# A fused attention and feed-forward layer: gate/up phases alternated with attention phases, segment by segment

## The chip, the core and the metric

The kernel runs on one core of a Trainium2 chip. A core has a tensor engine (PE, matrix products; its weight loads are listed as PEld), a vector engine (DVE), a scalar engine with lookup tables for functions such as exp (ACT), a general engine (POOL) and a queue engine (SP) that mainly issues transfers. Each engine works through its own instructions in order and waits on semaphores for the others. Matrix products land in PSUM, a small accumulator memory; everything else is in SBUF or in DRAM. The metric is the device time of one execution in microseconds. The profile names the clock that was granted to PE; it can be halved.

## The reference

The input is a sequence of 2048 rows of width 448. It is normalised, goes through a segmented attention with a recurrent memory (16 heads of width 28, 4 segments of 512 rows), and through a gated feed-forward block of inner width 1792; the two results are multiplied and added to the input.

```python
x = A_x
xn = _layernorm(x, axis=-1)
s = _A_ref(xn, A_wq, A_wk, A_wv, A_wo, A_beta)
g = _silu(_B_ref(xn, B_w_gate, B_w_up, B_w_down))
return x + s * g
```

Within `_A_ref`, for each segment (phi(t) is t + 1 for positive t, else exp(t)):

```python
p = _softmax(logits, axis=-1)
a_dot = jnp.einsum('bhqk,bhkd->bhqd', p, vs)
pq = phi(qs)
num = jnp.einsum('bhld,bhde->bhle', pq, M)
den = jnp.einsum('bhld,bhd->bhl', pq, z)[..., None] + 1e-06
a_mem = num / den
o = g * a_mem + (1.0 - g) * a_dot
outs.append(o)
pk = phi(ks)
M = M + jnp.einsum('bhld,bhle->bhde', pk, vs)
z = z + jnp.einsum('bhld->bhd', pk)
```

`logits` are the scaled products of queries and keys of the same segment with a causal mask, and `_B_ref` is `_gelu(x @ w_gate) * (x @ w_up) @ w_down`.

## The kernel before

Everything runs on tiles of 128 rows; a segment is four such blocks (`NB`), the 16 heads are four groups (`G`) of four heads padded to 32 columns, the inner width is 14 chunks (`NFC`).

The program is written as a sequence of tile operations, and a scheduler sets the order of the instructions on each engine. It may move work ahead of work that stands earlier in the code. Tiles come from pools with a fixed number of buffers; a new tile of a name waits until the oldest buffer of that name is free. PSUM has three pools of two buffers each: `ps_s` (two banks a tile: scores, or the gate and up products), `ps_pv` (P times V sums, or down sums) and `ps_m` (everything else, tiles named `m`).

The program has two halves. The first, lines 316 to 341, does the attention of all four segments:

- `layer_norm(s)`, line 127: statistics on DVE, the power -1/2 on POOL (L137), transposes on PE (L144).
- `project(s)`, line 172: queries and keys of each group (L182), values (L198), keys by row (L206), and the phi functions through ACT's exp (L189, L209).
- `scores` and `pv`, lines 239 and 261: for each group three steps over the key blocks. PE computes scores (L248), ACT the exp (L252), POOL the causal mask (L255), PE the product with the values (L266). The product of one step is issued after the scores of the next (`pend`).
- `evac`, line 274: DVE copies the sum out of PSUM (L276) and SP writes the row sums to DRAM (`den`).
- `memory_read(s, g)`, line 280: the read of the memory for a group (L282).
- `normalise(s)`, line 284: the row sums come back (`dc`), DVE forms the reciprocals (L292, L295), they go to DRAM (`rdr`) and come back broadcast over 128 partitions (`rb`, L302, one transfer of 256 KB for each group and side). POOL then multiplies and adds (L309 for segment 0; L312, L313, L314 for the others) and leaves the result in `oT`. A segment after the first has two sides, the softmax and the memory.
- `update(s)`, line 217: the memory gains the segment's keys and values.

The second half, the loop that starts at L350, is the feed-forward of all segments and the end: for each segment 14 pairs of gate and up products (L358), gelu on ACT (L361), the product on DVE (L362) into `hT`; then for each block the down products (L367), the wo products of the attention (L371), silu on ACT (L374), a product on DVE (L375), the sum with the input on POOL (L376), and one transfer out per segment. Between the halves stand a barrier and the reuse of the first half's SBUF. `oT` and `xnT` hold all four segments.

A guard, lines 148 to 168, computes from the weights whether the scores can overflow an exp without a maximum; if they could, a general path (not run with these inputs) computes the result.

## Time and profile before

| what | us |
|---|---|
| median of three runs | 378.45 |
| lowest and highest run | 376.80, 379.18 |
| the profiled execution | 377.6 |
| its span in the profile | 375.8 |
| mean granted clock of PE | 0.869 of full |

The profile covers one execution. Its span runs from the first to the last recorded activity; the execution's own time is 1.8 us longer. In a row of a timeline the first two numbers are start and duration in us, then come engine, line, operation, output and input tiles with sizes, and the number of instructions that were merged; in square brackets stands how long the engine was idle before and what ended it. Neighbouring matmuls overlap, so a matmul's cost in a dense stretch is the distance from start to start. In a row of the costliest groups the two numbers after the first bar are the group's busy time in us and the mean of one in ns. In a row of windows the columns are the window and its length, then for each engine the busy time and the number of instructions, then PE's granted clock, the share of the transfer engines that was busy and GB/s.

### The profile page before, as it was taken

The page shows a single profiled execution, that of the slowest core. Times are in us where ns is not written, and L with a number is a line of the kernel's source. Part 1 is how long each engine was busy: PE and PEld are TensorE (multiplying, and loading weights), DVE is VectorE, ACT ScalarE, POOL GpSimd, SP SyncE. Part 2 cuts the span into 40 slices and gives each one's busy share as a digit, 9 for nine tenths or more (in the row PEclk, how much of TensorE's full clock was granted, in tenths as well). Part 3 has the DMA queues.
Part 4 walks back from the last instruction along what each step waited for, and adds up shares of the span by engine and source line. Part 5 has one row for each costly group of instructions (what it writes and reads, how often), then busy time and mean ns, then how long its engine had stood idle before and what let it go on. Part 6 is the DMA issues. An engine that isn't in the chain of part 4 may idle for free. (4 is left out here: it accounts for less than half of the span.)

```text
span 375.8 us, 4396 instructions
## 1 busy us (share of the span) xinstructions
PE 308.9 (82%) x1619; PEld 128.8 (34%) x1620; DVE 159.6 (42%) x297; ACT 146.4 (39%) x203; POOL 142.0 (38%) x207
## 2 busy tenths in 40 slices
PE   0356999995998924898346999999999999999992
PEld 0122343331423402223212244454445444544450
DVE  6827976872537703248221134312341234123420
ACT  1000589663456632437333723413333333333330
POOL 9800456337333187624579405661003100310021
PEclk9999999995559965559855589999999999999998
DMA  8991010011000122000220012613000300010001
GB/s 210 253 314 54 2 50 4 5 57 63 5 3 4 48 102 88 5 1 13 92 101 37 7 37 101 161 35 98 2 0 2 98 1 2 0 50 2 0 0 57
DMA packets 16964, 20.30 MB, mean 54 GB/s; under 512 B 2616, under 2 KB 12344, under 8 KB 16936
## 3 DMA queue, kind: packets, MB, share of 16 engines
q1 hardware_dynamic: 15472, 18.75, 16.2%
q10 hardware_dynamic: 1432, 1.20, 1.5%
q8 instruction: 14, 0.23, 0.3%
q14 instruction: 14, 0.11, 0.1%
q0 software_dynamic: 32, 0.00, 0.0%
HBM read 17.66 MB, written 2.29 MB: 53 GB/s over the span
## 5 line engine op out<-in xcount | busy, mean ns | idle before, releaser
L252 ACT ACTIVATE pt<-s 128x1024 bf16<-128x1024 f32 (+1 forms) x96 | 81.8, 881 | 93.4 <-PE s L248 66.7
L255 POOL TENSOR_SCALAR_AFFINE_SELECT pt<-pt 128x256 bf16<-128x256 bf16 x128 | 52.9, 432 | 64.2 <-ACT pt L252 63.4
L362 DVE TENSOR_TENSOR hT<-gl,s 128x512 bf16<-128x512 bf16 x56 | 38.2, 687 | 63.5 <-ACT gl L361 63.5
L358 PE MATMUL s<-xnT,wg_sb 112*128 112x512 bf16 x224 | 58.8, 386 | 0.1
L358 PE MATMUL s<-xnT,wu_sb 112*128 112x512 bf16 x224 | 58.4, 384 | 0.0
L361 ACT ACTIVATE gl<-s 128x512 bf16<-128x512 f32 x56 | 33.1, 597 | 63.5 <-PE s L358 63.5
L376 POOL TENSOR_TENSOR o_out<-sl,x_sb 128x448 bf16<-128x448 f32 x16 | 16.5, 1034 | 105.1 <-DVE sl L375 102.7
L266 PE MATMUL pv<-pt,vaug 128*32 128x128 bf16 (+3 forms) x256 | 37.7, 378 | 21.6 <-POOL pt L255 21.1
L248 PE MATMUL s<-qT,kT 32*128 32x128 bf16 (+3 forms) x256 | 43.0, 361 | 7.2 <-POOL mbd L234 5.0
L367 PE MATMUL pv<-wd_sb,hT 128*128 128x448 bf16 x224 | 44.3, 352 | 0.0
L358 PEld LDWEIGHTS <-wg_sb 112*128 112x128 bf16 x224 | 22.2, 99 | 27.3 <-issue 2.1
L358 PEld LDWEIGHTS <-wu_sb 112*128 112x128 bf16 x224 | 22.1, 99 | 27.1 <-issue 1.3
L367 PEld LDWEIGHTS <-hT 128*128 128x128 bf16 x224 | 21.9, 98 | 20.7
L182 PE MATMUL m<-xnT,wq_pad 112*128 112x512 bf16 x64 | 22.3, 468 | 6.9 <-DVE qT L186 5.5
L266 PEld LDWEIGHTS <-vaug 128*32 128x32 bf16 x256 | 11.2, 97 | 49.0 <-issue 47.0
L375 DVE TENSOR_TENSOR sl<-sl,m 128x448 f32<-128x448 f32 x16 | 9.9, 621 | 37.5 <-PE m L371 18.8
L312 POOL TENSOR_TENSOR oU<-oU,rb 128x512 f32<-128x512 f32 x12 | 15.2, 1266 | 20.9 <-DVE hT L362 12.4
L276 DVE COPY oU<-m 128x512 f32<-128x512 f32 x12 | 8.2, 690 | 33.7 <-PE m L282 14.9
L182 PE MATMUL m<-xnT,wk_pad 112*128 112x512 bf16 x64 | 22.0, 454 | 0.2 <-ACT phq_e L189 0.2
L248 PEld LDWEIGHTS <-kT 32*128 32x128 bf16 x256 | 10.7, 95 | 31.8 <-issue 29.2
L276 DVE COPY oU<-pv 128x512 f32<-128x512 f32 x16 | 11.0, 689 | 22.3 <-PE pv L266 20.8
L374 ACT ACTIVATE sl<-pv 128x448 f32<-128x448 f32 x16 | 8.7, 544 | 26.8 <-PE pv L367 26.8
(72 smaller groups left out, 291.3 us busy)
## 6 DMA issues: line engine op xcount, KB each, us to landing
rb<-rdr SPq DMA_DIRECT2D x28, 256.0 KB
x_sb<-in_A_x_dram SPq DMA_DIRECT2D x8, 448.0 KB
out_dram<-o_out SPq DMA_DIRECT2D x4, 448.0 KB
wg_sb<-in_B_w_gate_dram SPq DMA_DIRECT2D x1, 1568.0 KB
wu_sb<-in_B_w_up_dram SPq DMA_DIRECT2D x1, 1568.0 KB
wd_sb<-in_B_w_down_dram SPq DMA_DIRECT2D x1, 1568.0 KB
den<-oU SPq DMA_DIRECT2D x28, 8.0 KB
wq_raw<-in_A_wq_dram ACTq DMA_DIRECT2D x1, 392.0 KB
```

Source lines behind the costliest of these rows:

```text
L182: nc.tensor.matmul(out=pr[:], lhsT=wpad[nm][:, c, g * HG:(g + 1) * HG, :].rearrange("p h d -> p (h d)"), rhs=xnT[:, c, s, :], start=(c == ...
L248: nc.tensor.matmul(out=sp[:, j, c0:c0 + n], lhsT=kT[s][r, g, kb * P:(kb + 1) * P], rhs=qT[s][r, g, kb * P:L], start=True, stop=True)
L252: nc.scalar.activation(out=pt[:, :, 0:w], in_=sp[:, :, 0:w], func=ACT.Exp, scale=scale)
L255: nc.gpsimd.affine_select(out=v, in_=v, pattern=[[0, 2], [1, P]], compare_op=ALU.is_ge, fill=0.0, base=0, channel_multiplier=-1)
L266: nc.tensor.matmul(out=acc[i * HP:(i + 1) * HP, kb * P:L], lhsT=va[:, kb, g * HG + i, :], rhs=pts[i // 2][:, i % 2, c0:c0 + n], start=(kb ...
L276: nc.vector.tensor_copy(out=t[:], in_=ps[:])
L312: nc.gpsimd.tensor_tensor(out=o_a[:], in0=o_a[:], in1=rb[0][:], op=ALU.mult)
L358: nc.tensor.matmul(out=gu[:, i, :], lhsT=w_sb[:, c, fc * P:(fc + 1) * P], rhs=xnT[:, c, s, :], start=(c == 0), stop=(c == NDC - 1))
L361: nc.scalar.activation(out=gl[:], in_=gu[:, 0, :], func=ACT.Gelu_apprx_tanh)
L362: nc.vector.tensor_tensor(out=hT[:, fc, :], in0=gl[:], in1=gu[:, 1, :], op=ALU.mult)
L367: nc.tensor.matmul(out=d_ps[:, 0:D], lhsT=hT[:, fc, b * P:(b + 1) * P], rhs=wd_sb[:, fc, :], start=(fc == 0), stop=(fc == NFC - 1))
L376: nc.gpsimd.tensor_tensor(out=o_out[:, b, :], in0=sl[:], in1=xr[:, b, :], op=ALU.add)
```

## The change

The code is reordered so that the feed-forward of a segment runs between and beside the attention phases. The new main loop, in full:

```diff
+        layer_norm(0)
+        for _, f in project_units(0):
+            f()
+        oki = guard()
+        flip("exp")
+        for s in range(NSEG):
+            if s + 1 < NSEG:
+                if s > 0:
+                    load_x(s + 1)
+                layer_norm(s + 1)
+            if s < NSEG - 1:
+                gate_up(s)
+                flip("gelu")
+            if s == 2:
+                ok = nc.values_load(oki[0:1, 0:1], min_val=0, max_val=1)
+            pre = [(0.22, lambda g=g: memory_read(s, g)) for g in range(G)] if s > 0 else []
+            lists = []
+            if s < NSEG - 1:
+                lists.append(down_units(s))
+                lists.append(project_units(s + 1))
+            if s > 0:
+                lists.append(finish_units(s - 1))
+            if s < NSEG - 1:
+                pre.append((0.9, lambda: update(s)))
+            attention(s, pre + merge(*lists))
+            flip("exp")
+            normalise(s)
+        gate_up(NSEG - 1)
+        dn, fi = down_units(NSEG - 1), finish_units(NSEG - 1)
+        for b in range(NB):
+            for _, f in dn[3 * b:3 * b + 3] + fi[b:b + 1]:
+                f()
```

So segments 0, 1 and 2 have a gate/up phase, then an attention phase with fill; segment 3 has its attention directly after that of segment 2, and its gate/up behind it. `merge` interleaves the lists of units by their shares of the total; `attention` puts units between the steps:

```diff
+                    for pr in range(2):
+                        pts.append(scores(s, g, bk, pr))
+                        if pr == 0 and pend is not None:
+                            pend()
+                        n += 1
+                        while fill and done < tot * n / (6 * G):
+                            c, f = fill.pop(0)
+                            f()
+                            done += c
```

The units are the projections of the next segment (one unit for each L182, L198 and L206 group of before), the down products in pieces of five matmuls, and the end of the segment before (`finish_units`: wo products, product with the gate, sum with the input, and now one transfer in and one out per block). A down accumulator takes a `ps_m` tile in segments 0 to 2, and a `ps_pv` tile in segment 3. Silu is replaced by tanh, with the factor one half moved into `igate`:

```diff
-        nc.vector.tensor_scalar(out=igate[:], in0=igate[:], scalar1=1.0, scalar2=None, op0=ALU.add)
+        nc.vector.tensor_scalar(out=igate[:], in0=igate[:], scalar1=1.0, scalar2=2.0,
+                                op0=ALU.add, op1=ALU.mult)
...
-                sl = work.tile([P, D], F32, name="sl")
-                nc.scalar.activation(out=sl[:], in_=d_ps[:, 0:D], func=ACT.Silu)
-                nc.vector.tensor_tensor(out=sl[:], in0=sl[:], in1=a_ps[:, 0:D], op=ALU.mult)
-                nc.gpsimd.tensor_tensor(out=o_out[:, b, :], in0=sl[:], in1=xr[:, b, :], op=ALU.add)
...
+                    th = work.tile([P, D], F32, name="th")
+                    nc.scalar.activation(out=th[:], in_=d_ps[:, 0:D], func=ACT.Tanh, scale=0.5)
+                    t = blk.tile([P, D], F32, name="sg")
+                    nc.vector.scalar_tensor_tensor(out=t[:], in0=th[:], scalar=1.0,
+                                                   in1=d_ps[:, 0:D], op0=ALU.add, op1=ALU.mult)
```

ACT's functions are kept in phases: every exp of an attention phase is ordered behind the gelus before it and ahead of those after it.

```diff
+        def act(kind, **kw):
+            ins = nc.scalar.activation(**kw)
+            ins = getattr(ins, "ins", ins)
+            for p_ in prev["gelu" if kind == "exp" else "exp"]:
+                tc.add_manual_dep(ins, p_, ORDER, reason="one table at a time")
+            phase[kind].append(ins.name)
```

At the start, w_up goes to ACT's queue and w_gate stands directly ahead of the second segment's input on SP's; the guard moves behind the projections of segment 0; several memsets move from DVE to POOL and cover only the padding. `xnT`, `oT` and `hT` hold one or two segments instead of four, `oup` has 4 buffers instead of 5 for each side, and `pkb` one instead of two. The barrier between the halves is gone.

How this moves the instructions is shown at three places, before first and then now.

DVE at the start. BN_STATS on `x_sb` are the statistics of a segment's blocks, L140 and L193 the normalising, L145 and L198 the copies of the transposes, L186 and L217 those of the projections. Before:

```order
L140 TENSOR_SCALAR xn<-x_sb,mv,rstd 128x448
L168 TENSOR_REDUCE oki<-okh 1x1
L140 TENSOR_SCALAR xn<-x_sb,mv,rstd 128x448
L145 COPY xnT<-m 112x4x128 x2
L132 BN_STATS st<-x_sb 128x6 x2
L133 BN_AGGR mv<-st 128x2
L186 CAST qT<-m 128x512
```

Now (the fifth BN_STATS on DVE, the first of segment 1, is the second row):

```order
L193 TENSOR_SCALAR xn<-x_sb,mv,rstd 128x448 x2
L185 BN_STATS st<-x_sb 128x6
L198 COPY xnT<-m 112x4x128
L193 TENSOR_SCALAR xn<-x_sb,mv,rstd 128x448
L198 COPY xnT<-m 112x4x128
L193 TENSOR_SCALAR xn<-x_sb,mv,rstd 128x448
L198 COPY xnT<-m 112x4x128
L186 BN_AGGR mv<-st 128x2
```

The statistics of segment 1 stood behind the transposes of segment 0 and ahead of its projections; now the first of them stands ahead of the copies of the transposes.

POOL at the change from segment 1 to segment 2. The normalise operations of segment 1 are L312 to L314 before, L352 to L354 now; AFFINE_SELECT is the causal mask of segment 2. Before:

```order
L314 TENSOR_TENSOR oT<-oU_1011,oU_991 128x512
L312 TENSOR_TENSOR oU_1277<-oU_1277,rb_1310 128x512
L255 AFFINE_SELECT pt<-pt 128x2x128
L313 TENSOR_TENSOR oU_1058<-oU_1058,rb_1312 128x512
L255 AFFINE_SELECT pt<-pt 128x2x128
L314 TENSOR_TENSOR oT<-oU_1277,oU_1058 128x512
L255 AFFINE_SELECT pt<-pt 128x2x128 x24
```

Now:

```order
L354 TENSOR_TENSOR oT<-oU_1689,oU_1299 128x512
L352 TENSOR_TENSOR oU_1810<-oU_1810,rb_1844 128x512
L353 TENSOR_TENSOR oU_1304<-oU_1304,rb_1846 128x512
L354 TENSOR_TENSOR oT<-oU_1810,oU_1304 128x512
L295 AFFINE_SELECT pt<-pt 128x2x128 x2
L275 TENSOR_TENSOR macc<-macc,rb_2136 128x512
L276 CAST mbd<-macc 128x512
L295 AFFINE_SELECT pt<-pt 128x2x128 x4
```

The masks stood between the normalise operations; now all twelve normalise operations of segment 1 stand ahead of the first mask of segment 2.

PE at the wo products of segment 2 (L371 before, L398 now; the rows LDWEIGHTS are the weight loads, and `oT` is what normalise leaves). Before, where the first wo products of the program stand:

```order
L358 LDWEIGHTS wu_sb
L358 MATMUL s<-xnT,wu_sb 128x512
L371 LDWEIGHTS oT
L371 MATMUL m<-wo_sb,oT 128x448
L371 LDWEIGHTS oT
L371 MATMUL m<-wo_sb,oT 128x448
```

Now, in the attention of segment 3:

```order
L398 LDWEIGHTS oT
L398 MATMUL m<-wo_sb,oT 128x448
L305 LDWEIGHTS vaug_151
L305 MATMUL pv<-pt,vaug_151 32x256
L305 LDWEIGHTS vaug_151
L305 MATMUL pv<-pt,vaug_151 32x256
L288 LDWEIGHTS kT
L288 MATMUL s<-qT,kT 128x256
L398 LDWEIGHTS oT
L398 MATMUL m<-wo_sb,oT 128x448
```

The wo products stood in the feed-forward half, among gate and up products; those of segment 2 now stand among the last scores and P times V products of segment 3.

More of the change, by code (lines that the diff above doesn't have):

```diff
@@ L208, in project @@
[L208 to L215 removed]
+                    u.append((0.75, lambda b=b: ktok(b)))
@@ L363, in fast_path @@
-            o_out = op_.tile([P, NB, D], out.dtype, name="o_out")
-            for b in range(NB):
-                d_ps = ps_pv.tile([P, L], F32, name="pv")
-                for fc in range(NFC):
-                    nc.tensor.matmul(out=d_ps[:, 0:D], lhsT=hT[:, fc, b * P:(b + 1) * P],
-                                     rhs=wd_sb[:, fc, :], start=(fc == 0), stop=(fc == NFC - 1))
+                act("gelu", out=gl[:], in_=gu[:, 0, :], func=ACT.Gelu_apprx_tanh)
+                nc.vector.tensor_tensor(out=hT[s][:, fc, :], in0=gl[:], in1=gu[:, 1, :], op=ALU.mult)
```

402 lines of the change are left out of this document (218 added, 184 removed).

## The prediction

> **What bounds the kernel now.** I read the page first: the busy shares, the forty slices and the chain that ended last.
>
> ```profile
> span 375.8 us, 4396 instructions
> PE 308.9 (82%) x1619; PEld 128.8 (34%) x1620; DVE 159.6 (42%) x297; ACT 146.4 (39%) x203; POOL 142.0 (38%) x207
> PE   0356999995998924898346999999999999999992
> PEclk9999999995559965559855589999999999999998
> GB/s 210 253 314 54 2 50 4 5 57 63 5 3 4 48 102 88 5 1 13 92 101 37 7 37 101 161 35 98 2 0 2 98 1 2 0 50 2 0 0 57
> PE s L358 26%; PE pv L367 11%; PE m L371 3%; POOL o_out L376 1%; DVE sl L375 0%; PE pv L266 0%; POOLq L729 0%; DVEq L375 0%
> ```
>
> There are two halves. From about 215 us the tensor engine (PE) is full and at full clock: the feed-forward stage, priced by the chain. Before that, attention and projections leave PE with gaps and a halved clock.
>
> ```profile
> 221.65 20.72 PE s L358 x96
> 242.38 5.30 PE pv L367 x28
> 254.11 0.76 PE m L371 x4
> ```
>
> A gate/up matmul costs 20.72/96 = 0.216 us, a down matmul 5.30/28 = 0.189, four wo matmuls 0.76. A segment's gate/up is 112 x 0.216 = 24.2 us, its down 56 x 0.189 = 10.6, its wo 3.0. None of this gets cheaper.
>
> The stages of the first half, by windows (us; busy time of PE, PEld, DVE, ACT, POOL; granted clock):
>
> ```profile
> 47.00:75.00 28.00, 26.64 (x188) 10.60 (x186) 20.26 (x43) 22.54 (x30) 14.78 (x34) 1.00 0.08 20
> 100.00:110.00 10.00, 10.00 (x50) 2.40 (x51) 2.79 (x7) 6.14 (x8) 3.32 (x8) 0.50 0.00 1
> 175.00:200.00 25.00, 12.62 (x82) 4.75 (x84) 8.74 (x14) 9.45 (x12) 16.80 (x20) 0.70 0.23 86
> ```
>
> With projections to fill it PE is dense (first row); with only attention left (175 to 200) it is half idle. What holds it then is POOL, seen in the PE timeline:
>
> ```profile
> 35.64 0.39 PE L248 MATMUL s<-qT,kT 32*128 32x512 bf16 x1
> 37.25 1.04 PE L182 MATMUL m<-xnT,wq_pad 112*128 112x512 bf16 x4
> 38.12 1.03 PE L182 MATMUL m<-xnT,wk_pad 112*128 112x512 bf16 x4
> 49.38 0.43 PE L144 MATMUL m<-ident,xn 128*112 128x128 bf16 x4
> 54.39 0.41 PE L248 MATMUL s<-qT,kT 32*128 32x512 bf16 x4
> 59.82 0.39 PE L248 MATMUL s<-qT,kT 32*128 32x512 bf16 x1
> 81.82 1.07 PE L223 MATMUL m<-vaug,pkb 128*128 128x128 bf16 x16
> 83.37 0.39 PE L266 MATMUL pv<-pt,vaug 128*32 128x512 bf16 x2
> 87.36 0.61 PE L266 MATMUL pv<-pt,vaug 128*32 128x512 bf16 x2 [3.60 <-POOL pt L255]
> 110.44 1.89 PE L182 MATMUL m<-xnT,wq_pad 112*128 112x512 bf16 x4
> 114.02 1.04 PE L182 MATMUL m<-xnT,wq_pad 112*128 112x512 bf16 x4
> ```
>
> At 87.36 a P times V matmul had waited 3.60 us for the causal mask (L255), and the clock is half for the next 25 us (four matmuls take 1.89 at 110.44, 1.04 at 114.02). POOL was late because the normalise steps stand in its queue. That chain, for segment 3 (evacuation, reciprocal input, transfers, then POOL):
>
> ```profile
> 214.62 0.69 DVE L276 COPY oU<-pv 128x512 f32<-128x512 f32 x1 [4.04 <-PE pv L266]
> 218.80 0.25 DVE L292 TENSOR_SCALAR dc<-dc,igate 128x64 f32<-128x64 f32 x1 [3.48 <-DMA dc<-den]
> 221.57 6.74 SPq L302 DMA_DIRECT2D rb<-rdr  x5
> 226.51 1.27 POOL L312 TENSOR_TENSOR oU<-oU,rb 128x512 f32<-128x512 f32 x1 [12.37 <-DVE hT L362]
> 229.14 1.27 POOL L313 TENSOR_TENSOR oU<-oU,rb 128x512 f32<-128x512 f32 x1 [1.36 <-DMA rb<-rdr]
> 247.38 1.27 POOL L314 TENSOR_TENSOR oT<-oU,oU 128x512 bf16<-128x512 f32 x1
> rb<-rdr SPq DMA_DIRECT2D x28, 256.0 KB
> ```
>
> From the end of the copy (215.3) to the end of the last L314 (248.65) it is 33.3 us: 11.2 of round trips through DRAM, then 22.1 for the four groups, where L313 waits for its broadcast. Eight of 256 KB in 21 us is 100 GB/s, the rate that the slices show then. With competition it took longer, segment 2:
>
> ```profile
> 167.44 0.69 DVE L276 COPY oU<-pv 128x512 f32<-128x512 f32 x1
> 203.09 1.27 POOL L314 TENSOR_TENSOR oT<-oU,oU 128x512 bf16<-128x512 f32 x1
> ```
>
> 204.4 - 168.1 = 36.2 us. This chain is what decides my forecast: the change does not shorten it, and now hangs it between stages of PE.
>
> **The change, part by part.**
>
> Start. Vector-engine order again puts segment 1's statistics ahead of segment 0's work, so DVE waits for that load:
>
> ```profile
> 29.28 1.15 DVE L132 BATCH_NORM_STATS2 st<-x_sb 128x6 f32<-128x448 bf16 x2 [7.22 <-DMA x_sb<-in_A_x_dram]
> 31.15 1.87 PE L182 MATMUL m<-xnT,wq_pad 112*128 112x512 bf16 x4 [5.46 <-DVE qT L186]
> 47.44 0.93 PE L206 MATMUL m<-wk_raw,xnT 112*128 112x448 bf16 x4
> ```
>
> Now x(1) stands behind only w_gate on SP's queue (2.6 MB with its first half), and ACT's queue carries as much; 5.2 MB at 250 GB/s is 21 us, with latency 23 (estimate), against 29. But the order then wants x(2) too, at some 31 us. Projection(0) ran to 48.3; I take 45, two gate/up tiles already inside. Behind it: guard and transposes 3, twelve tiles of 8 x 0.216 = 20.7, part of update 0.5, DVE's extra 2. End of gate/up(0): **71** (66 to 78). The memsets moved to POOL lie under this load.
>
> Attention with fill. A group of attention alone: 54.39 to 59.82 is 5.43 us, less seven projection matmuls at 0.216, 3.9; four are 15.7 (lower bound). Upper: 35.64 to 83.7 is 48.1 us, less eleven units at 0.87 (37.25 to 38.12), sixteen of 0.76 (priced as wo, same columns), transposes 4 x 0.43, update 1.0: 23.6. That includes waits for ACT, which has slack in the longer phase, so I take 17.5. Fill of segment 0: down 10.6, next projections 8 x 0.87 + 8 x 0.76 = 13.0, update 0.6: phase **42**. Of segments 1 and 2: also wo 3.0, memory reads 0.9 partly earlier, update 1.0: phase **46**.
>
> Silu as tanh. The ACT row barely changes; DVE gains sixteen operations:
>
> ```profile
> L374 ACT ACTIVATE sl<-pv 128x448 f32<-128x448 f32 x16 | 8.7, 544 | 26.8 <-PE pv L367 26.8
> L375 DVE TENSOR_TENSOR sl<-sl,m 128x448 f32<-128x448 f32 x16 | 9.9, 621 | 37.5 <-PE m L371 18.8 <-ACT sl L374 15.9 <-PEq L729 2.8
> L361 ACT ACT_TABLE_LOAD x4 | 5.1, 1283 | 5.9 <-PE s L358 5.8
> ```
>
> 16 x 0.62 = 9.9 us under PE, DVE being 42% busy; without that cover each would delay its PSUM tile. Only the last lies on the end: 0.6. Table loads go from nine to eight; each 1.28 us lies under two gate/up tiles (3.4 us of PE).
>
> Gate/up(1) and (2): 24.2 + transposes 1.7 + memory reads 0.4 = 26.3. The gelu waits (one table at a time) hold nothing else back: ACT has no other work there. Extra small transfers (x per block, out per block) cost SP some 0.5 us each in issue; behind a late out stands the next den, one attention step at most, hidden.
>
> Normalise(0) has one side, four broadcasts: under gate/up(1). Normalise(1) has 33.3 us against 26.3. POOL's order puts all twelve operations ahead of attention(2)'s first mask, and DVE's order puts two memory-read copies into gate/up(2) that wait for buffers freed by L354. So the first P times V of attention(2) comes at T1 + 36 (33.3, then copy, update and two masks), not at 26.3 + 3: a stall of some 7 us in pieces, and a clock that may halve as at 87.36. For that I take 4 us (0 to 12, the 25 us there at half rate).
>
> Attention(3) follows attention(2) with no gate/up between, and PE's order puts wo(2) ahead of the last P times V. So it lasts normalise(2), 33.3, then four wo and the last group, half clock: 8. Then normalise(3), 33.3, against gate/up(3) 24.2 + one down 2.65: again a stall. Then wo 0.76, three downs with wo 3 x 3.41, 1.7 for a cold clock: 12.7.
>
> The end: the last feed-forward matmul before stood at about 368.4 (365.0, the last row of the chain's PE, and 3.4 of a block), so 7.4 to the end, in which
>
> ```profile
> 369.20 1.03 POOL L376 TENSOR_TENSOR o_out<-sl,x_sb 128x448 bf16<-128x448 f32 x1 [2.38 <-DVEq L729]
> ```
>
> is followed by 5.6 us of output. The new one is 112 KB instead of 448, plus 0.6 on DVE: I keep 7.4.
>
> Sum: 71 + 42 = 113; + 26.3 = 139.3; + 46 = 185.3 (T1); + 36 = 221.3; rest of attention(2) 46 - 3.3 + 4 = 46.7: 268; + 41.3 = 309.3; + 33.3 = 342.6; + 12.7 + 7.4 = 362.7. The profiled execution took 377.6 with a span of 375.8: + 1.8 is **364**, against a median of 378.45 that lies 0.9 above that execution.
>
> The Trainium skill, TensorE: Matmul & The Clock Gate, section What's actually happening, says the clock is full again after one busy window of about 3.4 us. The row 100 to 110 shows PE busy for all of 10 us at clock 0.50, so the measurement decides. By the page the half-clock terms would be 1.7 rather than 4, and the sum 362.
>
> **The rivals.**
>
> PSUM tiles run short (the slower side). In an attention phase a down accumulator keeps one of two `m` tiles through three units, so 56 other units share one. A k unit keeps it for a 0.54 exp, perhaps 1.0 of queue, 0.3 and 0.62 on DVE: 2.5 us; the next unit comes about 1.6 us later (one down unit 0.95, scores, PV). At worst 0.9 a unit. From 0.33 us a unit the gain is gone by over 1% (364 + 18 = 382); at 0.6 it is 398. Against it: the queue on ACT is often short, and orders interleave. Chance 0.15.
>
> The clock stays half through attention(2) and again in (3), as for 25 us after 87.36: 8 more in the one, 2 to 6 in the other: 374 to 378. Chance 0.13.
>
> All dense: attention at 15.7 and no clock loss: 3 x 1.8 + 4 + 1.7 + 1 = 12 less, 352; with the broadcasts also at the 250 GB/s of the first slices the chain would take 11 + 15.2 of POOL and save 7 at three places: 343. For it, only that nothing else moves data then; against it, the same 100 GB/s in the quiet stage after 221. Chance 0.12, of which 0.08 for under 345.
>
> **How the numbers follow.** My forecast, 352 to 373 around 364, has 0.60. Faster by over 1% (under 374.7): 0.60 + 0.12 + half of the clock rival, 0.06: 0.78. Slower by over 1%: most of the PSUM rival, 0.12. Within 1%: 0.10. One per cent is about what a measurement here can tell from no change. The range leaves out 0.08 below 345 and some 0.10 above 386.
>
> **What would show it.** Right: POOL idle for DMA rb among L352 to L354, then two masks and PE's longest wait at the start of attention(2); attention(3) about 40 us with PE mostly idle; a wait on oT before the last wo; attention(0) and (1) near 42 and 46 us at clock 1.00. Wrong: attention phases of 55 us with PE waiting on DVE or ACT for `m`; clock 0.50 while the phases are filled; gate/up(0) ending beyond 78; a normalise chain of 25 us, or attention(3) of 30.

## The result, and the profile after

The changed kernel takes 360.8 us (median of four runs, 360.2 to 361.5), the kernel before, run beside it, 377.7: the ratio is 0.955, with a 95% interval of 0.951 to 0.959. The forecast was 364, in a range of 345 to 386. The profiled execution took 360.19 us, its span is 358.3.

The head of the page after: the span, the busy time of each engine, and two of the rows with forty slices.

```profile
span 358.3 us, 4443 instructions
PE 296.1 (83%) x1618; PEld 122.0 (34%) x1620; DVE 159.3 (44%) x306; ACT 145.9 (41%) x202; POOL 140.4 (39%) x221
PE   0119999999999998999999488999988549999192
PEclk9999999999999999999999869999995556999788
```

Before, the tensor engine (PE) had 308.9 us of busy time in a span of 375.8, so 66.9 idle; now it has 296.1 in 358.3, so 62.2 idle. Of the 17.5 us that the span lost, 12.8 are busy time, though the matmuls are the same: they run at a full clock more of the time (the mean granted clock rose from 0.869 to 0.926). Only 4.7 are gaps that went. The low stretches of the two rows now stand at three places: about slice 23 (gate/up(2), from 200 us), slices 30 to 33 (attention(3)), and slices 38 to 40 (the end).

Those places by windows (length, busy time of PE, PEld, DVE, ACT and POOL, granted clock, DMA share, GB/s), first two filled attention phases, then the three low stretches:

```profile
80.00:90.00 10.00, 9.98 (x64) 3.52 (x62) 5.85 (x10) 6.51 (x9) 3.15 (x8) 1.00 0.01 2
160.00:170.00 10.00, 9.93 (x65) 3.91 (x64) 5.80 (x10) 5.51 (x7) 3.65 (x9) 1.00 0.09 25
200.00:210.00 10.00, 4.65 (x11) 1.53 (x11) 3.17 (x5) 0.60 (x1) 7.24 (x6) 0.64 0.27 100
280.00:290.00 10.00, 4.88 (x26) 1.06 (x25) 2.58 (x4) 4.73 (x6) 9.92 (x11) 0.50 0.27 98
330.00:335.00 5.00, 1.40 (x7) 0.41 (x5) 0.62 (x1) 0.54 (x1) 3.73 (x3) 1.00 0.26 98
```

With down and projection products between its steps attention keeps PE full at clock 1.00. In each low stretch the DMA share is 0.26 or 0.27 and the rate about 100 GB/s: there the broadcasts of a normalise step are running. They are what POOL waits for in the groups of the page (busy, mean ns, then idle time and its cause), while POOL's masks (L295) now hold PE for little:

```profile
L352 POOL TENSOR_TENSOR oU<-oU,rb 128x512 f32<-128x512 f32 x12 | 15.2, 1268 | 25.5 <-DMA rb<-rdr 25.0
PE pv L305 <- POOL pt L295: 5.1, 6, 2.7
```

The second row is of the waits (total, times, longest). Before, the same wait was 21.1 us.

The timelines show how a normalise chain stops PE in gate/up(2). The rows are of the vector engine (DVE) and PE; the brackets hold the idle time and what ended it.

```profile
184.26 0.68 DVE L315 COPY oU<-pv 128x512 f32<-128x512 f32 x1
202.29 0.69 DVE L315 COPY oU<-m 128x512 f32<-128x512 f32 x1 [6.09 <-POOL oT L354]
203.63 1.86 PE L364 MATMUL s<-xnT,wg_sb 112*128 112x512 bf16 x4 [5.11 <-DVE hT L368]
207.59 0.69 DVE L315 COPY oU<-m 128x512 f32<-128x512 f32 x1 [4.01 <-POOL oT L354]
216.97 1.27 POOL L354 TENSOR_TENSOR oT<-oU,oU 128x512 bf16<-128x512 f32 x1
```

Attention(1) ends with the copy at 184.26 (T1 = 184.94). DVE's copies of the memory reads (L315) want buffers that only L354 frees; behind them in DVE's order stands the product L368 that gate/up needs, and PE stands for 5.11 us. The chain ends at 218.24, T1 + 33.3.

### The profile page after: what moved, and what is told of

It reads as the page before. It is cut to its first block, busy times and chain, and to the rows that moved or that the text cites. A ratio compares the mean times of both kernels' runs of the same rounds, so it can differ in the third digit from the quotient of the medians.

```text
span 358.3 us, 4443 instructions
## 1 busy us (share of the span) xinstructions
PE 296.1 (83%) x1618; PEld 122.0 (34%) x1620; DVE 159.3 (44%) x306; ACT 145.9 (41%) x202; POOL 140.4 (39%) x221
## 3 DMA queue, kind: packets, MB, share of 16 engines
q10 hardware_dynamic: 1896, 2.81, 3.0%
## 5 line engine op out<-in xcount | busy, mean ns | idle before, releaser
L295 POOL TENSOR_SCALAR_AFFINE_SELECT pt<-pt 128x256 bf16<-128x256 bf16 x128 | 52.4, 426 | 85.2 <-ACT pt L142 84.0
L364 PE MATMUL s<-xnT,wg_sb 112*128 112x512 bf16 x224 | 61.3, 391 | 7.2 <-DVE hT L368 7.2
L142 ACT ACTIVATE gl<-s 128x512 bf16<-128x512 f32 x56 | 33.4, 597 | 74.7 <-PE s L364 74.7
L368 DVE TENSOR_TENSOR hT<-gl,s 128x512 bf16<-128x512 bf16 x56 | 38.3, 685 | 43.5 <-ACT gl L142 43.3
L288 PE MATMUL s<-qT,kT 32*128 32x512 bf16 (+3 forms) x256 | 39.7, 328 | 4.8 <-ACT pt L142 3.6
L377 PE MATMUL m<-wd_sb,hT 128*128 128x448 bf16 x168 | 39.6, 354 | 0.1
L305 PE MATMUL pv<-pt,vaug 128*32 128x512 bf16 (+3 forms) x256 | 31.6, 334 | 6.4 <-POOL pt L295 5.1
L364 PEld LDWEIGHTS <-wg_sb 112*128 112x128 bf16 x224 | 22.0, 100 | 34.2 <-issue 11.0
L377 PEld LDWEIGHTS <-hT 128*128 128x128 bf16 x224 | 20.3, 100 | 22.7 <-issue 7.0
L197 PE MATMUL m<-ident,xn 128*112 128x128 bf16 x64 | 7.2, 246 | 23.7 <-DVE xn L193 23.7
L398 PE MATMUL m<-wo_sb,oT 128*128 128x448 bf16 x64 | 17.5, 398 | 9.3 <-POOL oT L354 8.2
L352 POOL TENSOR_TENSOR oU<-oU,rb 128x512 f32<-128x512 f32 x12 | 15.2, 1268 | 25.5 <-DMA rb<-rdr 25.0
L315 DVE COPY oU<-m 128x512 f32<-128x512 f32 x12 | 8.0, 683 | 35.3 <-POOL oT L354 35.3
L403 POOL TENSOR_TENSOR o_out<-sg,xr 128x448 bf16<-128x448 f32 x16 | 16.5, 1034 | 15.6 <-DVE sg L401 15.4
L190 POOL TENSOR_TENSOR rstd<-rstd,nhalf 128x2 f32<-128x2 f32 x8 | 5.6, 703 | 40.1 <-DVE rstd L188 40.1
L353 POOL TENSOR_TENSOR oU<-oU,rb 128x512 f32<-128x512 f32 x12 | 15.2, 1266 | 11.7 <-DMA rb<-rdr 11.7
L213 PE MATMUL m<-xnT,wq_pad 112*128 112x512 bf16 x64 | 18.3, 409 | 0.9 <-DVE xnT L198 0.8
```

The lines of the kernel that those rows point to most:

```text
L142: ins = nc.scalar.activation(**kw)
L213: nc.tensor.matmul(out=pr[:], lhsT=wpad[nm][:, c, g * HG:(g + 1) * HG, :].rearrange("p h d -> p (h d)"), rhs=xnT[s][:, c, :], start=(c == ...
L288: nc.tensor.matmul(out=sp[:, j, c0:c0 + n], lhsT=kT[s][r, g, kb * P:(kb + 1) * P], rhs=qT[s][r, g, kb * P:L], start=True, stop=True)
L295: nc.gpsimd.affine_select(out=v, in_=v, pattern=[[0, 2], [1, P]], compare_op=ALU.is_ge, fill=0.0, base=0, channel_multiplier=-1)
L305: nc.tensor.matmul(out=acc[i * HP:(i + 1) * HP, kb * P:L], lhsT=va[:, kb, g * HG + i, :], rhs=pts[i // 2][:, i % 2, c0:c0 + n], start=(kb ...
L352: nc.gpsimd.tensor_tensor(out=o_a[:], in0=o_a[:], in1=rb[0][:], op=ALU.mult)
```

## The experiments

Two theories were set against each other. Theory N: from the end of attention(1) on, three stretches are as long as a normalise chain (T1 to the start of attention(2); attention(3); the end), because other work is tied to the chain; filling the attention phases is what brought the gain. Rival P: the tensor engine's own work, its PSUM tiles, its clock or the exponentials set these lengths.

The stages of each kernel's profiled execution stand here together. T1, T2 and T3 are the ends of the last accumulator copy of attention(1), (2) and (3), read from the DVE timelines; the last columns are the medians of the runs and their ratio to the kernel before, run on the same chip.

| kernel | T1 | T1 to T2 | T2 to T3 | T3 to end of span | span | median | ratio to before, 95% |
|---|---|---|---|---|---|---|---|
| after | 184.9 | 78.3 | 42.1 | 53.0 | 358.3 | 360.8 | 0.951 to 0.959 |
| e1_k16 | 184.4 | 76.1 | 47.6 | 42.7 | 350.8 | 353.6 | 0.934 to 0.945 |
| e3_bufs | 185.0 | 75.1 | 41.7 | 53.2 | 355.1 | 357.6 | 0.942 to 0.957 |
| e4_late | 185.8 | 78.4 | 39.9 | 57.7 | 361.8 | 362.0 | 0.955 to 0.967 |
| e9_dmask3_bufs | 187.0 | 75.2 | 40.7 | 53.7 | 356.6 | 358.1 | 0.942 to 0.950 |
| e11b_wo | 185.5 | 74.9 | 40.0 | 54.2 | 354.7 | 356.4 | 0.937 to 0.950 |
| e11_both | 184.9 | 74.7 | 36.1 | 53.6 | 349.4 | 353.1 | 0.931 to 0.947 |
| e13_third_tie | 185.5 | 74.7 | 29.4 | 57.3 | 346.8 | 347.3 | 0.914 to 0.930 |
| e10_dmask23_k16_bufs | 184.8 | 74.1 | 38.2 | 43.0 | 340.0 | 341.8 | 0.897 to 0.908 |
| e12_all | 185.2 | 74.1 | 42.6 | 43.8 | 345.7 | 347.0 | 0.913 to 0.926 |

### Which part of the change brings the gain

**e2_nofill**: in the code the units stand after the attention instead of between its steps.

```diff
-            attention(s, pre + merge(*lists))
+            attention(s, pre)
+            for _, f in merge(*lists):
+                f()
```

> The changed kernel with its alternating phases, buffers and tanh, but the down, wo and next-segment projection units run after each attention phase instead of between its steps (memory reads and the memory update stay ahead). Theory N (the gain comes from filling the attention phases): the attention phases are half empty again, at a lower granted clock, while the units then run by themselves; each of attention(0), (1), (2) with its units takes 10 to 14 us more, less what the normalise chain hides of it, since units that come after the attention now cover part of that chain: 375 to 395 us, that is, the whole gain or more is gone. Rival (alternating the phases is what gains, the filling isn't): 357 to 365 us.

Its four runs took 390.4, 405.8, 406.2 and 409.0 us, all above the kernel before (374.3 to 378.4 there). The shortest lies inside what I expected; the other three lie above it, with a lower mean clock (0.846 to 0.848 against 0.893). They spread too much for a ratio, and the profile is of one of the three long ones (406.15), so its clock is no measure of the shortest. One window of its attention(0), and the page's clock row:

```profile
90.00:100.00 10.00, 9.26 (x41) 2.50 (x41) 2.42 (x5) 7.14 (x10) 4.21 (x11) 0.64 0.01 2
PEclk9999999995799897555899589999997555599977
```

The attention phases are not empty in e2: the scheduler moved part of the units back between the steps. In attention(0) (71.2 to 105.5) stand 43 of the 120 matmuls that fill it in the changed kernel (19 of L213, 24 of L377). So e2 tests less filling, not none. The kernel before also had projections between the steps of its attention phases, as the prediction counts them. What the runs show: with the phases alternated but less filled, the kernel is slower than the one before, by 3.6% in its shortest run (390.4 against a median of 377.0), so the order of the phases by itself is not the gain, and the changed kernel cannot do without the filling. How the gain grows with the filling they don't show. The edits at the start (queues, guard, memsets) are in e2 too; they were not run alone.

**b1_tanh** puts the tanh alone into the kernel before; **e5_silu** takes it out of the changed kernel and puts the scalar engine's Silu back (the scale of the output gate goes from 2 to 1 with it).

```diff
-                nc.scalar.activation(out=sl[:], in_=d_ps[:, 0:D], func=ACT.Silu)
+                nc.scalar.activation(out=th[:], in_=d_ps[:, 0:D], func=ACT.Tanh, scale=0.5)
+                nc.vector.scalar_tensor_tensor(out=sl[:], in0=th[:], scalar=1.0,
+                                               in1=d_ps[:, 0:D], op0=ALU.add, op1=ALU.mult)
```

> The kernel before with one part of the change alone: silu written as tanh with one more vector operation per block. Theory N (the order of the phases brings the gain, the tanh only makes it possible): within 1% of the kernel before, 374 to 380 us. Rival (tanh itself saves time: table loads and waits in the feed-forward stage go): eight loads of 1.28 us less, up to 10 us, 367 to 372.

> The changed kernel with the scalar engine's Silu instead of tanh and a vector operation. Theory N: the twelve silus that now lie inside attention phases each need one table load and another one back, 2.6 us in which no exponential is made, some 10 us of the 42 to 46 us of a phase; the scalar engine is busy for about 24 of these, so about half of it is hidden, but each gap makes the tensor engine wait 1 to 2 us and may cost the clock: 364 to 376 us. Rival (the loads all lie in slack): 358 to 363. Rival (the waits drop the clock for whole phases): over 380.

b1_tanh: 378.2 us, ratio 1.002 (0.999 to 1.005): no difference, as Theory N had it. e5_silu: 375.8 us, ratio 0.998 (0.994 to 1.002): 15 us more than the changed kernel, at the edge of what I expected. The groups of table loads, of e5_silu (first two rows) and of the changed kernel (third):

```profile
L142 ACT ACT_TABLE_LOAD x19 | 24.4, 1283 | 1.1 <-PE s L288 0.8
L381 ACT ACT_TABLE_LOAD x13 | 16.7, 1283 | 0.5 <-PE m L377 0.2
```

```profile
L142 ACT ACT_TABLE_LOAD x7 | 9.0, 1283 | 0.1
```

With one more load elsewhere in each, that is 33 loads against 8: 25 x 1.283 = 32 us on the scalar engine, of which 15 come through. They come where the attention is: attention(0) takes 48.1 instead of 41.8 us, T2 to T3 46.5 instead of 42.1. So the tanh is worth nothing by itself and nearly the whole gain once silu stands between exponentials. Neither of the two parts pays alone.

### What sets the three stretches

**e1_k16**: each 256 KB broadcast, over 4 heads x 32 partitions, as four transfers of one head.

```diff
-                    nc.sync.dma_start(
-                        out=r[:],
-                        in_=rdr[side, g * HG:(g + 1) * HG, :].unsqueeze(1).to_broadcast([HG, HP, L]))
+                    for i in range(HG):
+                        nc.sync.dma_start(
+                            out=r[i * HP:(i + 1) * HP, :],
+                            in_=rdr[side, g * HG + i, :].unsqueeze(0).to_broadcast([HP, L]))
```

> The changed kernel, with each 256 KB broadcast of a reciprocal row (one transfer over 4 heads x 32 partitions) written as four transfers of one head over 32 partitions each; same bytes, same arithmetic. Theory N (the normalise chain of 33 us sets three stretches, and it is paced by broadcasts that move at 100 GB/s): the four broadcast pairs go faster, the chain falls from 33 to about 27 us (11 of round trips, then POOL's twelve steps of 1.27 us, or the 32 transfer issues on SP's queue), and each of the three stretches shrinks by 5 to 6: about 345 us (340 to 350). Rival P (the tensor engine, its PSUM tiles and the exponentials bound the attention phases, the chain only fills the same time): 358 to 362, with the chain shorter and the stretches as long as before. If the transfers still move at 100 GB/s, the limit is not in the shape of the transfer, and the time stays at 361.

353.6 us: between the two theories, in the range of neither. Its window and timelines, after attention(1) (first two rows), after attention(2) (two), and at the end (four):

```profile
195.00:200.00 5.00, 5.00 (x25) 2.29 (x24) 2.01 (x3) 1.69 (x3) 4.17 (x4) 1.00 0.47 141
191.17 15.62 SPq L343 DMA_DIRECT2D rb<-rdr  x32
266.60 25.99 SPq L343 DMA_DIRECT2D rb<-rdr  x32
284.39 0.59 PE L321 MATMUL m<-pqT,mbd 128*128 128x512 bf16 x1 [4.33 <-DVE oU L315]
323.93 1.26 POOL L353 TENSOR_TENSOR oU<-oU,rb 128x512 f32<-128x512 f32 x1 [8.49 <-DMA rb<-rdr]
338.58 1.26 POOL L355 TENSOR_TENSOR oT<-oU,oU 128x512 bf16<-128x512 f32 x1
330.47 5.27 PE L378 MATMUL pv<-wd_sb,hT 128*128 128x448 bf16 x27
339.90 0.55 PE L399 MATMUL m<-wo_sb,oT 128*128 128x448 bf16 x2 [3.21 <-POOL oT L355]
```

The shape of the transfer was the limit: the rate rises from 100 to 141 GB/s and the DMA share from 0.26 of sixteen engines (4.2 of them) to 0.47. Now the issue of 32 transfers (15.62 us, 0.49 each) and POOL's own twelve steps (12 x 1.26 = 15.1) are about equally long, and at the end the twelve steps take 15.9 us (323.93 to 339.84), 1.33 each, instead of 21.3 in the changed kernel (317.70 to 338.99). The Trainium skill, DMA: Bandwidth & Descriptors, section Why a DMA increments its semaphore by 16 and not by 1, says that a transfer is spread over the largest number of engines, up to sixteen, that divides the outermost dimension on both of its sides; here these were the 4 heads and the 128 partitions, which gives four, and the trace agrees with its 0.26.

Gate/up(2) runs through without a stop, and the first scores of attention(2) come at 208.0 instead of 219.7. But T2 comes only 2.8 us earlier, and T2 to T3 even grows by 5.5: the order that was built for this kernel puts attention's masks among POOL's normalise steps, so the chain waits for attention there and attention for the chain (the broadcasts of segment 2 take 26 us to issue, for want of free buffers, and PE waits 4.33 us for a copy). A faster chain does not help where the work stays tied to it.

At the end, T3 to the end of the span falls by 10.3 us, but little of that is the chain: from T3 it takes 31.8 us (308.09 to 339.84) instead of 33.7, since its first step comes 15.8 us after T3 instead of 12.4. The other 8.4 us lie behind it. The new order puts all 56 down products of segment 3 ahead of the wait for the last `oT` (the 27 at 330.47 are the last large group), where the changed kernel has 42 of them behind it. So e1 changed two things, the transfers and the scheduler's order, and most of its gain at this place is the order. The down products moved ahead, with the broadcasts as before, was not run.

**e3_bufs**: eight buffers for the memory-read copies, in a pool of their own (two tiles of the start move to another pool to make room).

```diff
         oup = pool("oup", 4)
+        oup1 = pool("oup1", 8)
...
-            t = oup.tile([P, L], F32, name=f"oU{side}")
+            t = (oup1 if side else oup).tile([P, L], F32, name=f"oU{side}")
```

> The changed kernel with eight instead of four buffers for the memory-read copies, so that the copies that DVE makes in gate/up(2) don't wait for the normalise steps of segment 1. Theory N: the 5.1 and 1.7 us waits of the tensor engine in gate/up(2) go, gate/up(2) takes 27 instead of 36.8 us, and attention(2) starts some 8 us earlier; its masks then stand behind the last normalise step of segment 1 (34 us after the end of the attention before), so the tensor engine waits there for 4 to 6 us: net gain 2 to 5 us, 356 to 359. Attention(3) and the end don't change. Rival P (no such limit by the chain): the whole 8 to 10 us are gained, 351 to 353. Rival clock (the new wait falls into attention, where the clock stays at a half for 20 us and more): 361 to 368.

357.6 us, as Theory N had it. The PE waits in gate/up(2) are gone, the first scores behind it come at 208.7 instead of 219.7, and the wait stands in attention(2) instead (a row of the PE timeline, and a window):

```profile
219.16 0.97 PE L306 MATMUL pv<-pt,vaug 128*32 128x512 bf16 x4 [5.54 <-POOL pt L296]
215.00:220.00 5.00, 0.84 (x4) 0.21 (x3) 0.99 (x2) 0.23 (x1) 4.06 (x5) 0.65 0.04 9
```

11 us of gate/up(2) became 3 us of T2. The masks (L296) stand behind the last normalise step on POOL, and the product waits for them until T1 + 34.1.

**The ties of attention(3).** Five kernels take away, in turn, what ties attention(3) to the chain of segment 2. e4_late emits wo(2) behind gate/up(3) in the changed kernel (four of its sixteen products stayed in attention(3), since the order of the engines is built by estimates):

```diff
-            if s > 0:
+            if 0 < s < NSEG - 1:
                 lists.append(finish_units(s - 1))
...
         gate_up(NSEG - 1)
+        for _, f in finish_units(NSEG - 2):
+            f()
```

> The changed kernel with segment 2's wo products and outputs taken out of attention(3) and put behind gate/up(3). Theory N: attention(3) is held by the masks, which stand behind the normalise steps of segment 2 in POOL's queue, not by the wo products on the tensor engine; so attention(3) keeps its 40 to 42 us, and what it gains is that 3 us of wo now lie where the tensor engine waits for the last normalise: 357 to 362 us. Rival (the tensor engine's order, with wo products that wait for oT in the middle of attention, is what stretches attention(3)): attention(3) falls to 30 us or less and the time to 348 to 352.

362.0 us: attention(3) shrinks by 2.1 us, and the last stretch grows by 4.7. That is the upper end of what Theory N expected, but with four products left in place it tells little against the rival.

e9_dmask3_bufs, on top of the eight buffers, makes the masks of attention(3) on DVE (`tri` is a 128x128 triangle of ones and zeros):

```diff
+                if s == NSEG - 1:
+                    nc.vector.tensor_tensor(out=v, in0=v, in1=tri[:].unsqueeze(1).to_broadcast([P, 2, P]),
+                                            op=ALU.mult)
+                    continue
                 nc.gpsimd.affine_select(out=v, in_=v, pattern=[[0, 2], [1, P]],
```

> The changed kernel with eight buffers for the memory-read copies (as in e3_bufs) and with the causal masks of attention(3) made by the vector engine (a product with a triangle of ones and zeros) instead of POOL, so that they don't stand behind the normalise steps of segment 2 in POOL's queue. Broadcasts as before. Theory N: attention(3) is then held only by the wo products of segment 2, which come 33 us after the end of attention(2), and by its own length of 29 us alone; it takes 30 to 37 instead of 42 us, and the rest of the kernel moves up with it: 345 to 353 us against 357.6 for the eight buffers alone. Rival P (attention(3) is as long as its own work at the low clock, or as the exponentials make it): 356 to 360.

358.1 us, the same as e3_bufs: my expectation failed, and the rival's number came. But the PE timeline of e9 doesn't show the rival's cause:

```profile
280.13 0.93 PE L407 MATMUL m<-wo_sb,oT 128*128 128x448 bf16 x2 [2.94 <-POOL oT L363]
285.85 0.93 PE L407 MATMUL m<-wo_sb,oT 128*128 128x448 bf16 x2 [2.75 <-POOL oT L363]
291.20 0.93 PE L407 MATMUL m<-wo_sb,oT 128*128 128x448 bf16 x2 [3.55 <-POOL oT L363]
296.59 0.93 PE L407 MATMUL m<-wo_sb,oT 128*128 128x448 bf16 x2 [2.50 <-POOL oT L363]
```

PE is stopped four times, 5.5 us apart, once for each group of the chain: the wo products stand in its order ahead of the next steps of attention, and wait for oT. One tie was taken away, another holds the same stretch. That gave the next pair: wo(2) held back until five tiles of gate/up(3) are issued (by a dependency without a wait, written into the order), without and with the masks moved.

```diff
+                if s == NSEG - 1 and fc == 4:
+                    mark.append(getattr(ins, "ins", ins).name)
+                    for _, f in finish_units(s - 1):
+                        f()
...
+                    if s == NSEG - 2:
+                        tc.add_manual_dep(getattr(ins, "ins", ins), mark[0], ORDER, reason="wo late")
```

> The changed kernel with eight buffers for the memory-read copies (as in e3_bufs) and segment 2's wo products held back until five tiles of gate/up(3) have been issued; the masks stay on POOL. With e3_bufs (neither), e9_dmask3_bufs (masks alone) and e11_both this makes a table of two by two. Theory N (two ties, each enough by itself to hold attention(3) until the normalise chain of segment 2 ends): the masks of the second half of attention(3) still stand behind the last normalise step, 33 us after attention(2); attention(3) stays at 38 to 42 us: 354 to 359 us. Rival (the wo products alone were the tie): 344 to 350.

> As e11b_wo, and with the masks of attention(3) on the vector engine too, so that neither masks nor wo products wait for the normalise chain of segment 2 inside attention(3). Broadcasts as before. Theory N: attention(3) falls to its own length, 29 to 32 instead of 41 us, and the end moves up with it, since the last chain starts earlier: 344 to 350 us. Rival P (attention(3) is as long as its own work at the low clock): attention(3) stays at 38 to 41 us and the time at 355 to 359.

e11b_wo: 356.4 us, attention(3) 40.0. e11_both: 353.1 us (351.2 to 356.7), attention(3) 36.1, not the 29 to 32 I expected. The DVE timeline of e11_both shows a third tie:

```profile
277.31 0.69 DVE L324 COPY oU<-pv 128x512 f32<-128x512 f32 x1 [1.22 <-POOL oT L363]
283.45 0.69 DVE L324 COPY oU<-pv 128x512 f32<-128x512 f32 x1 [4.13 <-POOL oT L363]
288.83 0.69 DVE L324 COPY oU<-pv 128x512 f32<-128x512 f32 x1 [3.94 <-POOL oT L363]
```

The copies out of the accumulator have four buffers, and those are held by segment 2 until its normalise step has read them. e13_third_tie gives them six:

```diff
-        oup = pool("oup", 4)
+        oup = pool("oup", 6)
```

> As e11_both, with six instead of four buffers for the copies out of the attention accumulator. In e11_both attention(3) still took 36.1 us, and its trace shows these copies waiting 4.13 and 3.94 us on the vector engine for normalise steps of segment 2, which hold the buffers. Theory N (this was the third tie of attention(3) to the chain, and the last): attention(3) falls to its own length, 26 to 31 us; the end moves up by 4 to 7 us, less what the last chain waits for POOL to finish segment 2 (POOL is busy with it until 34 us after attention(2)): 345 to 350 us against 353.1. Rival (what is left is attention(3)'s own work at half clock): attention(3) stays at 35 to 37 us, 352 to 354 us.

347.3 us, attention(3) 29.4. Its copies:

```profile
265.45 0.69 DVE L324 COPY oU<-pv 128x512 f32<-128x512 f32 x1 [0.50 <-PE pv L314]
272.21 0.69 DVE L324 COPY oU<-pv 128x512 f32<-128x512 f32 x1 [1.99 <-PE pv L314]
280.21 0.69 DVE L324 COPY oU<-pv 128x512 f32<-128x512 f32 x1 [2.61 <-POOL oT L363]
```

One wait of 2.61 us is left. So at this place Theory N holds and Rival P falls: attention(3) took 41.7 us with all three ties (e3_bufs), 40.7 without the masks, 40.0 without the wo products, 36.1 with the buffers alone and 29.4 with hardly any, with the same exponentials and still at half clock (0.50 from 270 to 290). What the phase would take at full clock stays open. In exchange the last chain, now closer behind that of segment 2 and its outputs, is longer (36.8 us instead of 34.2 in e3_bufs), and so is T3 to the end: 12.3 us of attention(3) became 8.3 of the span.

**e10_dmask23_k16_bufs** and **e12_all** put the pieces together. e10: broadcasts per head, eight buffers, masks of attention(2) and (3) on DVE. e12: also wo(2) held back, and both rows of a head in one transfer:

```diff
+                    for i in range(HG):
+                        nc.sync.dma_start(
+                            out=r2[i * HP:(i + 1) * HP, 0:ns, :],
+                            in_=rdr[0:ns, g * HG + i, :].unsqueeze(0).to_broadcast([HP, ns, L]))
```

> The changed kernel with all three at once: broadcasts in four transfers each (as in e1_k16), eight buffers for the memory-read copies, and the causal masks of attention(2) and (3) on the vector engine. Theory N: all that ties attention to the normalise chain from segment 1 on is loosened; gate/up(2) ends 24 us after attention(1), attention(2) takes 42 to 46, attention(3) 28 to 35, and the end comes some 43 us after it as in e1_k16: 322 to 340 us. Rival P (the tensor engine's work, its clock and the exponentials bound these stretches): 348 to 354, no more than e1_k16 gave.

> All loosened: masks of attention(2) and (3) on the vector engine, eight buffers, segment 2's wo products behind five tiles of gate/up(3), and the broadcasts per head as in e1_k16, but both rows of a head in one transfer (16 issues of 128 KB instead of 32 of 64 KB, so SP's queue issues them in about 8 instead of 15.6 us). Theory N: attention(3) is then 29 to 32 us instead of 38 in e10, and the last stretch becomes bound by the tensor engine (gate/up 24, wo 3, down 10.6, wo 3) instead of by the chain: 328 to 338 us against 341.8 of e10. Rival P: 338 to 344.

e10 takes 341.8 us, 0.902 of the kernel before (0.897 to 0.908) and 19 us less than the changed kernel: the best version found. Its T3 to the end, 43.0, has the same order of the down products as e1's (all 56 ahead of the last chain's end), so here too not all of the gain is the faster chain. The time is just above what I expected, since T2 stayed at 258.9 where I had 251 to 255, and T2 to T3 at 38. e12 takes 347.0, slower than e10, against my expectation, though sixteen issues take 12.9 us instead of 15.6 (I had 8; the median issue takes 0.42 us in both kernels, and part of the 12.9 are waits for POOL to free the buffers, 12.3 us over the whole kernel). The PE and DVE timelines of e12 show where it went, and one window of e12 and of e10 (fourth and fifth row) what differs:

```profile
288.52 1.26 PE L314 MATMUL pv<-pt,vaug 128*32 128x512 bf16 x16 [1.74 <-DVE oU L324]
295.86 0.69 DVE L324 COPY oU<-pv 128x512 f32<-128x512 f32 x1
301.18 0.69 DVE L324 COPY oU<-pv 128x512 f32<-128x512 f32 x1
290.00:295.00 5.00, 5.00 (x14) 1.76 (x13) 0.69 (x1) 0.97 (x2) 0.00 (x0) 0.53 0.00 0
290.00:295.00 5.00, 5.00 (x25) 2.33 (x24) 2.66 (x4) 1.34 (x3) 0.00 (x0) 1.00 0.01 2
```

The last P times V products start at 288.52, 29 us after T2, as expected. But the last two copies stand in DVE's order behind products of gate/up(3), which had been pulled forward into the gaps; T3 comes at 301.87, 12 us late, and with it the last chain. Work that fills a gap was here put ahead of work that a chain waits for. In e10 the last two copies stand behind products of gate/up(3) in the same way; they come earlier, at 290.79 and 296.35, because the last P times V products start 1.6 us earlier after T2 (286.53) and the gate/up products that follow run at full clock there and at about half in e12. Why the clock differs no run shows; e12 has no wo products in the gaps before. A version of e10 with more accumulator buffers, or with these copies put first, was not tried.

## Why the prediction came out right, step by step

- End of gate/up(0), 71: the first scores stand at 71.31. The load that DVE waits for had landed by 23.32 (I had 23), the first projection started at 26.74, and the projections ended at 45.3. The 45 was a choice and not a sum, so that part is luck.
- Attention with fill, 42 and 46: attention(0) took 41.8. Attention(1) took 47.1 from its first scores (137.79) to T1, and gate/up(1) before it 24.7 where I had 26.3; these two misses nearly cancel, and T1 was forecast as 185.3 and measured as 184.9. The 17.5 for attention's own work was picked inside bounds of 15.7 and 23.6. The reason given for it holds (PE was busy 40.8 of the 41.7 us from 71.31 to 113.0, so the waits are covered); that it fits within a microsecond is luck too. The clock was 1.00, and PE had no long wait for an `m` tile: the first rival did not occur.
- Silu as tanh, hidden: right for what I counted (DVE's sixteen operations), and e5_silu shows what I had not priced, namely what it would cost without.
- T1 to the first P times V of attention(2), 36: it ran at 223.93, T1 + 39.0. The chain ended at T1 + 33.3, as priced. I had named both of its ties, the copies in gate/up(2) and the masks of attention(2), and had the masks come last, with PE's longest wait at the start of attention(2); that sign did not come. In the trace it was the copies, which held gate/up(2) until 219.6, and the masks then waited for their exponentials. e3_bufs shows that the one stands behind the other: take the first away, and the second waits 5.54 us.
- Rest of attention(2), 46.7: measured 39.3 (223.93 to T2 = 263.24). This is the term that was mis-sized, by 7.4. Four were for a lost clock, which fell in gate/up(2) instead and was back before attention(2); 2.4 because the phase took 43.6 (from 219.68) and not 46; 1.0 because more of it lay ahead of the first product. With the 3.0 of the line above, T1 to T2 is 4.4 short of the forecast's 82.7, and this is the whole distance between its sum, 362.7, and the span of 358.3.
- The clock: I had set a rule of the Trainium skill (TensorE: Matmul & The Clock Gate, section What's actually happening: full again after one busy window of about 3.4 us) behind the row of the kernel before that spoke against it. The rows of after, by windows and the PE timeline, stand nearer to the rule. After the second wait of gate/up(2) PE is dense from 208.92 on; the mean of 0.69 from 210 to 215 means full clock from about 213, some 4 us later. What kept it at half for 25 us before, with PE as busy, no run here settles. The traces do show where it came back: in the kernel before at about 113.3, 3 us after attention's products, which have 32 rows or 32 columns, gave way to projections over 112 rows (110.44), and in e13 at about 291.4, 2 us after gate/up(3) had PE to itself (289.06). In the filled phases, where both kinds alternate, it stayed at 1.00. That the width of the products is the cause was not tested.

```profile
208.92 1.86 PE L364 MATMUL s<-xnT,wg_sb 112*128 112x512 bf16 x4 [1.72 <-DVE hT L368]
210.00:215.00 5.00, 5.00 (x17) 1.91 (x16) 0.69 (x1) 0.99 (x2) 3.79 (x3) 0.69 0.26 96
215.00:220.00 5.00, 5.00 (x24) 2.04 (x23) 2.06 (x3) 1.61 (x4) 2.53 (x2) 1.00 0.00 0
```

- Attention(3), 41.3: 42.1. Normalise(2) ended 33.1 us after T2, as the chain was priced. The reason I gave was the wo products in PE's order; the experiments show three ties that hold it (masks, wo, buffers), of which I had named one for this phase. Nor was PE mostly idle, as I had said: it was busy 30.0 of the 42.1 us, at a mean clock of 0.59.
- Normalise(3), 33.3, and the last wo and down, 12.7: measured 33.7 and 12.4. PE waited for oT before its last products, as forecast, and the first 14 down products behind the wait took 4.48 us where the next 14 took 2.81, which is the 1.7 that the sum has for a cold clock:

```profile
333.78 0.36 PE L398 MATMUL m<-wo_sb,oT 128*128 128x448 bf16 x1 [2.75 <-POOL oT L354]
339.05 0.56 PE L398 MATMUL m<-wo_sb,oT 128*128 128x448 bf16 x1 [4.90 <-POOL oT L354]
339.40 4.48 PE L377 MATMUL pv<-wd_sb,hT 128*128 128x448 bf16 x14
344.47 2.81 PE L377 MATMUL pv<-wd_sb,hT 128*128 128x448 bf16 x14
```

- The tail, 7.4: 6.9.
- The clock rival did not add to the sum, though attention(3) ran at 0.50 for most of its length: that lay under the chain. The all-dense rival's second half, broadcasts above 100 GB/s, is possible in this kernel, as e1_k16 shows, but not with this shape of transfer.

## What to carry to other kernels

A long chain on a side engine sets a stretch of the main engine through everything that is queued behind it or holds a buffer for it; count all such ties before expecting anything from removing one, since each can hold the same stretch when another is gone. When small units are interleaved with a phase that uses a function table, make them use the same table: the switch costs nothing in a phase of its own, and nearly the whole gain between exponentials. Read a gain as busy time and idle time apart: here most of it was the same matmuls at a better clock. And where a scheduler sets the order, an edit of one part can move work in another: compare the order of the instructions at the place where the time changed before putting the gain down to the edit.

## What the hardware did that I had not expected

Short DVE operations on bf16 data took two to three times as long beside POOL's f32 work. The rows: the same operation (L226, 128x512) of e10, at 215.96 beside a cast and a product of POOL and at 231.01 with POOL idle, and masks of e10 without POOL's normalise steps (four) and beside them (six); the last row is such a step, of e12:

```profile
215.96 0.69 DVE L226 TENSOR_SCALAR phq_e<-phq_e 128x512 bf16<-128x512 bf16 x1
231.01 0.29 DVE L226 TENSOR_SCALAR phq_e<-phq_e 128x512 bf16<-128x512 bf16 x1 [0.66 <-ACT phq_e L147]
255.72 1.08 DVE L301 TENSOR_TENSOR pt<-pt,tri 128x256 bf16<-128x256 bf16 x4
280.74 5.14 DVE L301 TENSOR_TENSOR pt<-pt,tri 128x256 bf16<-128x256 bf16 x6 [0.34 <-ACT pt L147]
218.17 1.71 POOL L361 TENSOR_TENSOR oU<-oU,rb 128x512 f32<-128x512 f32 x1
```

0.29 became 0.69, a mask 5.14/6 = 0.86 instead of 1.08/4 = 0.27, and POOL's step 1.71 instead of 1.27. The Trainium skill, SBUF — State Buffer, section Who interferes with whom, says that the two engines share a pair of ports, and that a DVE instruction with two SBUF inputs, as the masks are, contends with a POOL instruction that reads SBUF; the rows agree in kind.
